# Attention and MoE on one core: a third operand set for head 2, staging for heads 1 and 2 in the x ring, and other plan numbers

## The chip, the core and the metric

One Trainium2 chip, one of its cores. A core has TensorE (PE, with its weight loads shown as PEld), VectorE (DVE), ScalarE (ACT), GpSimd (POOL) and SyncE (SP), which here issues nearly all DMA transfers. The metric is the device time of the whole program in microseconds, from several runs; the profile comes from one execution.

## What is computed

The kernel is an attention layer with a block mask, followed by a two-layer MoE-like block, all in fp32:

```python
scores = scale * np.matmul(q, k.transpose(0, 1, 3, 2))      # 4 batches, 8 heads, 768 x 64
scores = np.where(mask, scores, -1000000000.0)              # blocks of 32: band, first, last, 3 drawn
scores = scores - np.max(scores, axis=-1, keepdims=True)
attn = np.exp(scores)
attn = attn / (np.sum(attn, axis=-1, keepdims=True) + 1e-09)
out = np.matmul(attn, v)
# x: 3072 tokens x 512 (heads side by side)
h = x @ w_in                                                # 512 x 2048
g = np.where(h >= 1, h, np.where(h <= -1, 0.0, (h + 1) ** 2 / 4.0))
y = g @ w_out                                               # 2048 x 512
```

The weights come as 64-bit floats, and the kernel turns their bits into fp32 on the chip ("conversion").

## The kernel before

There are 32 heads (4 batches of 8), and after each batch the MoE block of that batch, which runs beside the next batch's heads. A head works on 768 x 768 scores in 12 chunks of 128 keys by 384 queries (`scores`, `expo`, `values`); its row maxima come first, from 12 matmuls (`max_mm`) that DVE reduces (`max_red`), then a column of maxima (`max_col`), a transpose on PE (`max_turn`) and a row that ACT or DVE writes into the operand (`max_row`). To keep fp32 accuracy an operand is split into a rounded part and a residual: `hi` rounds the loaded 128 x 768 tile `qk` into `qkh` on ACT, `lo` subtracts, and DMA moves (`hi_one`, `hi_two`, `lo_two`) put the four pieces into `KA`, `QA`, `KB` and `QB`. `KA` and `QA` exist twice (`SETS = 2`) and also hold the mask rows; heads take them in turn. `qk` and `qkh` have one buffer, `KB` and `QB` two. The x ring (`xp`, 10 buffers of 128 x 2 x 384) holds the attention output that feeds the MoE block.

Heads 0 to 9 (`WHOLE`) multiply the probabilities by the values in plain fp32 (L360); later heads split the probabilities too (L203, L343, L362, L363). The first batch is "wide": it may use the accumulators `oa0` to `oa2` and `hp` of the MoE block, which are free then.

The conversion of the weights works on pieces of 128 x 1024: L175 on ACT, then L176, L177, L179 and L181 on DVE, then a rounding on ACT (L203) and a residual on DVE (L187). `w_in` has eight pieces and stays in `wi`; `w_out` has eight pieces, is used by the first MoE half as it is made (tile `w`) and kept in DRAM for the later ones.

The order is set by a plan: every step is put into a list with a number (`at(t, ...)`), in units of one chunk, 12 units a head. Head i starts at 12 i; the steps ahead of it and behind it stand at distances from tables: `P` for all, `PW` over it for the first batch, `PA` for the second, `PM` for the first MoE half. `CONV` and `CSTEP` place the `w_in` conversions. The list is sorted and recorded, and a scheduler makes each engine's order from it, with the number as priority. Each engine then runs its own queue in order.

## Time and profile before

| | before |
|---|---|
| time, median of 3 runs | 975.48 us (972.75 to 977.56) |
| the profiled execution's own time | 975.02 us |
| its span | 973.2 us |
| PE busy | 946.3 us (97%) |
| DVE busy | 728.3 us (75%) |
| ACT busy | 645.0 us (66%) |
| POOL busy | 245.6 us (25%) |
| mean DMA rate | 158 GB/s |

Busy time of PE is the union of its matmuls, whose ends are modelled: two matmuls that start 0.18 us apart show 0.34 us each. So the starts tell its pace, and the rows that name a wait tell where it stood. A stretch of the span is read for itself: an engine that is busy three quarters of the span can be full in one head and idle in the next.

### The profile page before, as it was taken

To read this page: it belongs to the slowest core of one execution; us is meant where nothing else is said; L and a number is where in the kernel's file an instruction comes from. 1 tells how busy PE (TensorE), PEld (TensorE's weight loads), DVE (VectorE), ACT (ScalarE), POOL (GpSimd) and SP (SyncE) were. 2 spreads that over 40 slices of the span, in tenths; PEclk is the share of its full clock that TensorE was granted. 3 is DMA by queue.
4 is the path that set the end of the run, shared out by engine and by line. 5 is a ranking of instruction groups with operands and counts; after the bars stand their busy time and mean duration, and the time that the engine had idled before them with its cause. 6 is when DMAs were issued, how large, how long until landed. Compare 5 with 4: busy or idle time off the path is not lost.

```text
span 973.2 us, 14591 instructions
## 1 busy us (share of the span) xinstructions
PE 946.3 (97%) x4746; PEld 832.7 (86%) x4746; DVE 728.3 (75%) x1317; ACT 645.0 (66%) x1304; POOL 245.6 (25%) x230
## 2 busy tenths in 40 slices
PE   6899999998999999999999999999999999999998
PEld 4577777887889999998998999899899999999997
DVE  6889887779998888889887878888787885422222
ACT  5587876687676767767676676767667667433433
POOL 2000000024443334334333343433434344000000
PEclk9899999999999999999999999999999999999999
DMA  7766676653364555544464544545455432433432
GB/s 210 207 193 201 194 241 219 226 190 115 130 187 144 159 160 147 169 134 137 141 187 150 152 128 133 174 149 158 150 151 162 144 96 92 157 126 130 162 130 98
DMA packets 56080, 154.08 MB, mean 158 GB/s; under 512 B 9594, under 2 KB 17934, under 8 KB 56004
## 3 DMA queue, kind: packets, MB, share of 16 engines
q1 hardware_dynamic: 55964, 153.11, 51.1%
q8 instruction: 38, 0.62, 0.3%
q14 instruction: 38, 0.31, 0.1%
q10 hardware_dynamic: 40, 0.03, 0.0%
HBM read 100.95 MB, written 14.81 MB: 119 GB/s over the span
## 4 chain that ended last, share of the span: by engine, by line
PE 83%; DVE 7%; DMA 4%; issue 2%; ACT 2%; SPq 0%; ACTq 0%; DVEq 0%
PE oa L512 8%; PE oa L514 8%; PE oa L513 8%; PE hp L484 7%; PE hp L486 7%; PE hp L485 7%; PE pa L279 6%; PE pa L330 5%; PE po L362 5%; PE pa L331 5%; PE po L363 4%; PE po L360 4%; PE oa L360 3%; DVE mc L284 2%; DMA qk<-in_qk_t_dram 2%
## 5 line engine op out<-in xcount | busy, mean ns | idle before, releaser
L350 POOL TENSOR_TENSOR acc<-acc,pt 128x384 f32<-128x384 f32 x176 | 195.2, 1109 | 233.9 <-ACT pt L335 200.9
L284 DVE TENSOR_REDUCE mc<-pa 128x1 f32<-128x384 f32 x384 | 201.6, 548 | 20.1 <-PE pa L279 15.2
L203 ACT CAST ph<-pt 128x384 fp32r<-128x384 f32 x264 | 135.7, 514 | 92.9 <-PE po L362 86.3
L343 DVE TENSOR_TENSOR pl<-pt,ph 128x384 fp32r<-128x384 f32 x264 | 156.1, 591 | 37.1 <-ACT ph L203 36.5
L335 ACT ACTIVATE pt<-pa 128x384 f32<-128x384 f32 x288 | 140.6, 489 | 54.4 <-PE pa L331 44.2
L484 PE MATMUL hp<-x,wi 128*128 128x384 f32 x448 | 156.6, 349 | 2.3 <-DVE r L496 2.2
L512 PE MATMUL oa<-w,gh 128*128 128x512 f32 x384 | 153.8, 401 | 0.3 <-ACT gh L203 0.3
L514 PE MATMUL oa<-w,gl 128*128 128x512 f32 x384 | 151.6, 395 | 0.0
L486 PE MATMUL hp<-x,wi 128*128 128x384 f32 x448 | 151.6, 338 | 0.0
L485 PE MATMUL hp<-x,wi 128*128 128x384 f32 x448 | 151.1, 337 | 0.0
L513 PE MATMUL oa<-w,gh 128*128 128x512 f32 x384 | 150.8, 393 | 0.0
L279 PE MATMUL pa<-KA,QA 88*128 88x384 f32 x384 | 139.5, 381 | 2.1 <-DMA QA<-qkh 0.6
L350 POOL TENSOR_TENSOR acc<-pt 128x384 f32<-128x384 f32 x44 | 45.1, 1025 | 344.8 <-ACT pt L335 344.8
L496 DVE SCALAR_TENSOR_TENSOR r<-r,hp 128x384 f32<-128x384 f32 x112 | 61.7, 551 | 84.6 <-ACT r L493 84.4
L505 DVE TENSOR_TENSOR gl<-r,gh 128x384 fp32r<-128x384 f32 x128 | 89.9, 702 | 26.0 <-ACT gh L203 25.5
L490 ACT ACTIVATE r<-hp,half_c 128x384 f32<-128x384 f32 x112 | 65.1, 582 | 54.6 <-PE hp L486 47.7
L330 PE MATMUL pa<-QA,KA 102*128 102x384 f32 x288 | 98.9, 343 | 1.3 <-DVE mc L284 0.9
L331 PE MATMUL pa<-QB,KB 128*128 128x384 f32 x288 | 97.9, 340 | 0.0
L362 PE MATMUL po<-ph,vn 128*128 128x384 f32 x264 | 91.1, 345 | 3.0 <-DVE xun L372 2.8
L484 PEld LDWEIGHTS hp<-x,wi 128*128 128x128 f32 x448 | 84.5, 189 | 8.2 <-DVE r L496 4.0
L279 PEld LDWEIGHTS pa<-KA,QA 88*128 88x128 f32 x384 | 73.4, 192 | 21.0 <-DVE mc L284 6.0
L363 PE MATMUL po<-pl,vn 128*128 128x384 f32 x264 | 88.8, 337 | 0.0
(103 smaller groups left out, 1619.4 us busy)
## 6 DMA issues: line engine op xcount, KB each, us to landing
w<-wo_dram SPq DMA_DIRECT2D x112, 512.0 KB
qk<-in_qk_t_dram SPq DMA_DIRECT2D x32, 384.0 KB
raw<-in_moe_w_in_dram SPq DMA_DIRECT2D x16, 512.0 KB
raw<-in_moe_w_out_dram SPq DMA_DIRECT2D x16, 512.0 KB
wo_dram<-w SPq DMA_DIRECT2D x16, 512.0 KB
lv<-in_v_dram SPq DMA_DIRECT2D x32, 192.0 KB
QB<-qkh SPq DMA_DIRECT2D x32, 192.0 KB
KB<-qkh SPq DMA_DIRECT2D x32, 192.0 KB
```

The lines of the kernel that those rows point to most:

```text
L279: nc.tensor.matmul(out=pm[:, 0:HALF], lhsT=QAi[0:KM, t * 128:(t + 1) * 128], rhs=KAi[0:KM, kh * HALF:(kh + 1) * HALF], start=True, stop=True)
L284: nc.vector.reduce_max(out=st["mc"][:, t, kh:kh + 1], in_=st.pop(("pm", t, kh))[:, 0:HALF], axis=AX.X)
L330: nc.tensor.matmul(out=ps[:, 0:HALF], lhsT=KAi[0:KA, ks], rhs=QAi[0:KA, cs], start=True, stop=False)
L331: nc.tensor.matmul(out=ps[:, 0:HALF], lhsT=st["KB"][:, ks], rhs=st["QB"][:, cs], start=False, stop=True)
L343: (nc.gpsimd if i < 2 * H and c in PL1 else nc.vector).tensor_tensor(out=pl, in0=st["p", c], in1=f(st["ph", c]), op=ALU.subtract)
L350: nc.gpsimd.tensor_tensor(out=st["acc", hf], in0=prev, in1=st["p", c], op=ALU.add)
L484: nc.tensor.matmul(out=hv, lhsT=wi[:, j, 0, fs], rhs=x[:, 0], start=(j == 0), stop=False)
L485: nc.tensor.matmul(out=hv, lhsT=wi[:, j, 0, fs], rhs=x[:, 1], start=False, stop=False)
L486: nc.tensor.matmul(out=hv, lhsT=wi[:, j, 1, fs], rhs=x[:, 0], start=False, stop=(j == NP - 1))
L512: nc.tensor.matmul(out=o, lhsT=gh[:, ts], rhs=w[:, 0], start=(fi == 0), stop=False)
L513: nc.tensor.matmul(out=o, lhsT=gh[:, ts], rhs=w[:, 1], start=False, stop=False)
L514: nc.tensor.matmul(out=o, lhsT=gl[:, ts], rhs=w[:, 0], start=False, stop=(fi == NF - 1))
```

## The change

The x ring is empty until the first heads are done. The change uses eight of its ten buffers before that: two become a third pair `QA[2]`, `KA[2]`, used by head 2 alone; heads 1 and 2 load their `qk` into two more, right behind the constants, round into two more, and head 2's `KB` and `QB` take the last two. Heads from 3 on take the two old sets in turn (`operand_set`). The constant rows of sets 1 and 2 are written by GpSimd in a step of their own, `other_sets`. The residual `lo` is done by GpSimd for heads 1, 3, 5 and 6 (`QL`) and by DVE for the others; before it was GpSimd for head 0 alone. Heads 0 to 3 get tables of their own (`P0` to `P3`), all other tables have other numbers, and the `w_in` conversions start a little later and stand 2 x 7.19 units apart instead of 2 x 6.297.

```diff
+    def wide_tile():
+        return xp.tile([128, 2, HALF], F32R, name="x").rearrange("p a c -> p (a c)")
+
+    QA.append(wide_tile())
+    KAt.append(wide_tile())
+
+    def operand_set(i):
+        return i if i < 3 else (i - 3) % 2
...
-        for i in range(SETS):
+        for i in range(SETS + 1):
             nc.gpsimd.memset(f(QA[i][64:128]), 0.0)
...
-        for i in range(1, SETS):
-            rounded(nc.gpsimd, KAt[i][64:KA], ef)
         nc.scalar.copy(out=idr, in_=idf)
+        shared["ef"] = ef
+
+    def other_sets():
+        for i in range(1, SETS + 1):
+            rounded(nc.gpsimd, KAt[i][64:KA], shared["ef"])
+        rounded(nc.gpsimd, QA[SETS][64:KM], f(QA[0][64:KM]))
...
-        G = {**P, **PW} if wide else {**P, **PA} if i < 2 * H else P
+        G = {**P, **PW, **(P0, P1, P2, P3, {})[min(i, 4)]} if wide else {**P, **PA} if i < 2 * H else P
...
-        QAi, KAi = QA[i % SETS], KAt[i % SETS]
+        QAi, KAi = QA[operand_set(i)], KAt[operand_set(i)]
...
-            st["x"] = ld.tile([128, S], F32, name="qk")
+            st["x"] = f(wide_tile()) if i in (1, 2) else ld.tile([128, S], F32, name="qk")
...
-            st["hi"] = tp.tile([128, S], F32R, name="qkh")
+            st["hi"] = wide_tile() if i in (1, 2) else tp.tile([128, S], F32R, name="qkh")
...
-            (nc.vector if i else nc.gpsimd).tensor_tensor(out=st["x"], in0=st["x"], in1=f(st["hi"]), op=ALU.subtract)
+            (nc.gpsimd if i in QL else nc.vector).tensor_tensor(out=st["x"], in0=st["x"], in1=f(st["hi"]), op=ALU.subtract)
...
-            st["KB"] = qk.tile([128, S], F32R, name="KB")
-            st["QB"] = qk.tile([128, S], F32R, name="QB")
+            st["KB"] = wide_tile() if i == 2 else qk.tile([128, S], F32R, name="KB")
+            st["QB"] = wide_tile() if i == 2 else qk.tile([128, S], F32R, name="QB")
...
-        at(-99 if i == 0 else pre - G["qs"] - G["ld"], load_qk)
+        at((-99, -89, -88)[i] if i < 3 else pre - G["qs"] - G["ld"], load_qk)
...
     at(TC, consts)
+    at(TC2, other_sets)
...
+P2 = {'qs': 28.491, 'ld': 9.372, 'vs': 8.581, 'm0': 9.353, 'm1': 4.82, 'mr': 0.376, 'mc': 4.207, 'mt': 3.273, 'mw': 1.003, 'lag': 3.06}
+QL = (1, 3, 5, 6)
...
-CONV, CSTEP = 8.526, 6.297
+CONV, CSTEP = 8.718, 7.19
```

What this does to the engines' queues is shown at three places. First SP, which issues the transfers, from the loads and moves of the first heads on. Before, behind the constants, head 0's moves and two weight loads, this stands in a row (`qk_181` and `qkh_233` are head 1's):

```order
L217 DMA lv_356<-in_v_dram 128x384
L221 DMA qk_181<-in_qk_t_dram 128x768
L168 DMA raw_372<-in_moe_w_in_dram 128x1024 x2
L231 DMA KA1_116<-qkh_233 64x768
L231 DMA QA1_114<-qkh_233 64x768
L231 DMA QB_245<-qkh_233 64x768
L231 DMA KB_244<-qkh_233 64x768
L249 DMA QB_245<-qk_181 64x768
L250 DMA KB_244<-qk_181 64x768
L168 DMA raw_539<-in_moe_w_in_dram 128x1024 x2
L221 DMA qk_282<-in_qk_t_dram 128x768
```

Now the same place, ahead of any weight load (`x_162` and `x_164` are the loads of heads 1 and 2, `x_180` the rounded tile of head 1; `qk_126` is head 0's):

```order
L236 DMA x_162<-in_qk_t_dram 128x768
L236 DMA x_164<-in_qk_t_dram 128x768
L246 DMA QB_175<-qkh_168 64x768
L246 DMA KB_174<-qkh_168 64x768
L264 DMA QB_175<-qk_126 64x768
L265 DMA KB_174<-qk_126 64x768
L232 DMA lv_196<-in_v_dram 128x384
L246 DMA KA1_116<-x_180 64x768
L246 DMA QA1_114<-x_180 64x768
L246 DMA QB_193<-x_180 64x768
L246 DMA KB_192<-x_180 64x768
L264 DMA QB_193<-x_162 64x768
```

Both loads went ahead of head 0's moves; head 1's moves follow at once, then head 1's `lv` load and head 2's six moves, and only then the first two weight loads, of which four stood among these transfers before.

Second, PE from the end of head 0 to head 1's first score. Before (`KA_116`, `QA_114` are head 1's set; `oa_390` receives its first scores):

```order
L360 MATMUL oa_352<-pl,vn 128x384
L360 MATMUL oa_352<-pt,vn 128x384
L279 MATMUL pa<-KA_116,QA_114 128x384
L360 MATMUL oa_352<-ph,vn 128x384
L279 MATMUL pa<-KA_116,QA_114 128x384 x2
L360 MATMUL oa_352<-pl,vn 128x384
L279 MATMUL pa<-KA_116,QA_114 128x384 x6
L294 MATMUL pa<-idr,mr 1x128 x6
L330 MATMUL oa_390<-QA_114,KA_116 128x384
```

Now (`oa_396` receives head 1's first scores):

```order
L294 MATMUL pa<-KA_116,QA_114 128x384
L345 MATMUL oa_372<-QA_113,KA_115 128x384
L346 MATMUL oa_372<-QB,KB 128x384
L375 MATMUL oa_380<-pt,vn 128x384
L345 MATMUL oa_382<-QA_113,KA_115 128x384
L309 MATMUL pa<-idr,mr 1x128 x6
L346 MATMUL oa_382<-QB,KB 128x384
L375 MATMUL oa_380<-ph,vn 128x384
L345 MATMUL hp<-QA_113,KA_115 128x384
L346 MATMUL hp<-QB,KB 128x384
L375 MATMUL oa_380<-pl,vn 128x384
L345 MATMUL oa_396<-QA_114,KA_116 128x384
```

Head 1's maxima moved from the end of head 0 to its middle: the transposes stand among head 0's last scores, and three of head 0's last values come behind head 1's first score.

Third, DVE between head 8's last reduction and head 9's first. Before:

```order
L181 SCALAR_TENSOR_TENSOR cva_1753<-raw_1541,cva_1753 128x1024
L288 TENSOR_TENSOR mr_1525<-mc_1444 128x6
L399 RECIPROCAL rc_1512<-rc_1512 24x32
L240 TENSOR_TENSOR qk_1504<-qk_1504,qkh_1571 128x768
L176 TENSOR_SCALAR cva_1901<-cva_1901 128x1024
L177 TENSOR_SCALAR cva_1901<-cva_1901 128x1024
L179 SCALAR_TENSOR_TENSOR cva_1901<-raw_1635,cva_1901 128x1024
L181 SCALAR_TENSOR_TENSOR cva_1901<-raw_1635,cva_1901 128x1024
L187 TENSOR_TENSOR w_1819<-cva_1753,w_1819 128x512
```

Now:

```order
L191 TENSOR_SCALAR cva_1579<-cva_1579 128x1024
L303 TENSOR_TENSOR mr_1517<-mc_1436 128x6
L192 TENSOR_SCALAR cva_1579<-cva_1579 128x1024
L194 SCALAR_TENSOR_TENSOR cva_1579<-raw_1447,cva_1579 128x1024
L414 RECIPROCAL rc_1503<-rc_1503 24x32
L196 SCALAR_TENSOR_TENSOR cva_1579<-raw_1447,cva_1579 128x1024
L255 TENSOR_TENSOR qk_1486<-qk_1486,qkh_1565 128x768
L191 TENSOR_SCALAR cva_1718<-cva_1718 128x1024
L192 TENSOR_SCALAR cva_1718<-cva_1718 128x1024
L194 SCALAR_TENSOR_TENSOR cva_1718<-raw_1541,cva_1718 128x1024
L202 TENSOR_TENSOR w_1638<-cva_1579,w_1638 128x512
L196 SCALAR_TENSOR_TENSOR cva_1718<-raw_1541,cva_1718 128x1024
```

Two whole conversions stand here where one and a rest stood, and the piece of `w` in it is the first of the second weights; before it was the third.

## Rows read from the trace of the kernel before

**Rows 1.** The page, part 2: busy tenths of PE in 40 slices of the span

```profile
PE   6899999998999999999999999999999999999998
```

**Rows 2.** Chain that ended last, in order of time: start us, us, what; 0 to 60

```profile
0.74 2.92 DMA qk<-in_qk_t_dram
...
27.30 5.70 DVE mc L284 x12
...
36.60 7.42 DMA QA<-qkh
...
46.13 0.18 PE oa L330
...
46.66 0.65 PE po L360 x2
```

**Rows 3.** Timeline of PE, 25 to 45: start us, us, instruction [idle before <-releaser]

```profile
25.67 0.69 PE L279 MATMUL pa<-KA,QA 88*128 88x384 f32 x3
...
29.45 2.65 PE L279 MATMUL pa<-KA,QA 88*128 88x384 f32 x6
34.26 0.52 PE L294 MATMUL pa<-idr,mr 128*1 128x128 f32 x6 [2.16 <-DVE mr L288]
36.61 0.69 PE L330 MATMUL oa<-QA,KA 102*128 102x384 f32 x1 [1.83 <-ACT QA L299]
...
44.16 0.76 PE L279 MATMUL pa<-KA,QA 88*128 88x384 f32 x3 [0.63 <-DMA QA<-qkh]
```

**Rows 4.** Stretches: us, busy of PE, PEld, DVE, ACT, POOL; PEclk, DMA share, GB/s

```profile
35.00:41.83 6.83, 5.22 (x13) 4.32 (x14) 6.09 (x7) 5.05 (x10) 0.00 (x0) 0.50 0.79 183
58.70:136.10 77.40, 76.52 (x340) 56.92 (x339) 65.63 (x114) 61.92 (x121) 0.00 (x0) 1.00 0.72 212
136.10:151.30 15.20, 14.95 (x70) 11.28 (x68) 13.95 (x23) 11.05 (x22) 0.00 (x0) 1.00 0.68 215
151.30:179.70 28.40, 27.87 (x135) 23.00 (x134) 18.98 (x35) 18.91 (x38) 0.00 (x0) 1.00 0.71 227
211.50:242.80 31.30, 28.64 (x152) 26.00 (x151) 31.23 (x54) 24.87 (x52) 12.85 (x10) 1.00 0.39 124
```

The stretches are cut at the first maximum matmul of a head: heads 3 to 7, 8, 9 and 11.

**Rows 5.** Who PE waited for, 200 to the end: us in total, times, longest

```profile
PE po L362 <- DVE xun L372: 2.8, 4, 0.9
PE hp L484 <- DVE r L496: 2.2, 2, 1.7
PE pa L305 <- DVE mr L288: 1.4, 5, 0.3
```

**Rows 6.** Timeline of DVE, 7 to 12.2

```profile
7.18 0.55 DVE L120 CAST QA<-pa 24x384 fp32r<-24x384 f32 x1 [0.68 <-PE pa L118]
...
8.63 3.35 DVE L284 TENSOR_REDUCE mc<-pa 128x1 f32<-128x384 f32 x7
```

**Rows 7.** The residual `lo`, line 240: duration ns min/median/max, first and last start

```profile
L240 DVE TENSOR_TENSOR qk<-qk,qkh x31: 883/952/1770, 20.9 to 763.3; 128x768 f32<-128x768 f32 x31
...
L240 POOL TENSOR_TENSOR qk<-qk,qkh x1: 2072/2072/2072, 6.1 to 6.1; 128x768 f32<-128x768 f32 x1
```

**Rows 8.** Groups of DVE, 44.16 to 151.3: instruction xcount | busy us, mean ns

```profile
L179 DVE SCALAR_TENSOR_TENSOR cva<-raw,cva 128x1024 int32<-128x1024 int32 x8 | 9.8, 1224 | 0.2
L181 DVE SCALAR_TENSOR_TENSOR cva<-raw,cva 128x1024 int32<-128x1024 int32 x8 | 9.6, 1198 | 0.0
...
L176 DVE TENSOR_SCALAR cva<-cva 128x1024 f32<-128x1024 f32 x8 | 5.4, 672 | 0.5 <-ACT cva L175 0.4
```

**Rows 9.** Tile `w`, 130 to 250: duration ns min/median/max, first and last start

```profile
L512 PE MATMUL oa<-w,gh x36: 388/397/692, 160.5 to 247.5; 128*128 128x512 f32 x36
...
L187 DVE TENSOR_TENSOR w<-cva,w x14: 671/684/1504, 129.5 to 242.9; 128x512 fp32r<-128x512 f32 x14
```

**Rows 10.** Timeline of POOL and DVE around 344

```profile
343.76 1.17 POOL L350 TENSOR_TENSOR acc<-acc,pt 128x384 f32<-128x384 f32 x1 [0.67 <-ACT pt L335]
...
343.98 1.77 DVE L240 TENSOR_TENSOR qk<-qk,qkh 128x768 f32<-128x768 f32 x1
```

More of the change, by code (lines that the diff above doesn't have):

```diff
@@ L85, in body @@
     wi = cst.tile([128, 4, 2, FF], F32R, name="wi")
+    def wide_tile():
[4 more added lines that the diff above has]
+        return i if i < 3 else (i - 3) % 2
+    shared = {}
     def consts():
         M = slice(64, KM)
-        for i in range(SETS):
+        for i in range(SETS + 1):
             nc.gpsimd.memset(f(QA[i][64:128]), 0.0)
@@ L566, in body @@
         for hf in range(2):
-            moe(begin[b] + hf * NF * p, p, b, hf, b == 0 and hf == 0)
+            moe(begin[b] + (DELAY2 if b == 0 else 0) + hf * NF * p, p, b, hf, b == 0 and hf == 0)
     for fq in range(2):
@@ L586 @@
-PW = {'vw': 3.518, 'r1': 3.404, 'r2': 4.789, 'qs': 12.911, 'vs': 8.37, 'ld': 5.876, 'm0': 7.378, 'm1': 4.661, 'mr': 0.204, 'mc': 2.414, 'mt': 1.76, 'mw': 1.144, 'ex': 0.241, 'ph': 1.21, 'pl': 1.598, 'ps': 0.916, 'ow': 0.264, 'ot': -2.699, 'oa': 1.883, 'ah': 0.402, 'al': 1.005, 'su': 0.223, 'de': 0.736, 'yw': 0.447, 'yy': 1.398, 'xm': 0.574, 'xh': 0.586, 'xl': 1.764, 'lag': 3.338}
+P = {'vw': 5.936, 'r1': 0.432, 'r2': 3.59, 'qs': 8.759, 'ks': 11.973, 'vs': 8.74, 'ld': 6.54, 'm0': 8.319, 'm1': 5.436, 'mr': 0.733, 'mc': 1.81, 'mt': 1.788, 'mw': 0.322, 'ex': 0.098, 'ph': 0.947, 'pl': 1.297, 'ps': 1.153, 'ow': 1.181, 'ot': 0.059, 'oa': 0.704, 'ah': 0.495, 'al': 0.487, 'su': 0.524, 'de': 1.45, 'yw': -0.311, 'yy': 1.616, 'xm': 0.512, 'xh': 0.797, 'xl': 2.852, 'gr': 0.112, 'gs': 0.335, 'gm': 0.748, 'gh': 0.844, 'gl': 1.475, 'l2': 1.536, 'l3': 0.137, 'l1': 0.132, 'cl': 8.876, 'cs': 2.804, 'cd': 1.518, 'co': 6.416, 'lag': 3.517}
@@ new lines @@
+PW = {'vw': 2.912, 'r1': 3.203, 'r2': 4.396, 'qs': 12.314, 'vs': 8.121, 'ld': 6.69, 'm0': 8.627, 'm1': 4.668, 'mr': 0.184, 'mc': 1.989, 'mt': 1.714, 'mw': 1.232, 'ex': 1.044, 'ph': 0.99, 'pl': 2.083, 'ps': 2.834, 'ow': 0.042, 'ot': -5.45, 'oa': 2.183, 'ah': -0.339, 'al': 1.56, 'su': 0.973, 'de': 5.555, 'yw': 0.289, 'yy': -1.207, 'xm': 0.389, 'xh': 1.951, 'xl': 2.771, 'lag': 3.428}
+P0 = {'qs': 14.014, 'vs': 7.862, 'vw': 4.385, 'lag': 3.653}
+P1 = {'qs': 21.286, 'ld': 7.496, 'vs': 10.037, 'm0': 11.05, 'm1': 4.665, 'mr': 0.533, 'mc': 5.247, 'mt': 3.948, 'mw': 2.561, 'lag': 2.771}
@@ L587 @@
+P2 = {'qs': 28.491, 'ld': 9.372, 'vs': 8.581, 'm0': 9.353, 'm1': 4.82, 'mr': 0.376, 'mc': 4.207, 'mt': 3.273, 'mw': 1.003, 'lag': 3.06}
+P3 = {'qs': 13.489, 'ld': 3.031, 'vs': 8.426, 'm0': 9.569, 'm1': 5.068, 'mr': 0.299, 'mc': 4.038, 'mt': 3.742, 'mw': 3.153, 'lag': 3.444}
+QL = (1, 3, 5, 6)
 TC = -90
+TC2 = -13.843
+DELAY2 = 0.0
 ONE = 12
-XLATE = 2.917
-H0 = 0.909
+XLATE = 3.793
+H0 = 0.512
 PH1 = ()
@@ L595 @@
 XL1 = ()
-PA = {'vw': 5.512, 'r1': 0.547, 'r2': 4.117, 'qs': 10.75, 'vs': 6.462, 'ld': 4.892, 'm0': 7.743, 'm1': 5.228, 'mr': 0.143, 'mc': 2.394, 'mt': 1.652, 'mw': 1.455, 'ex': 0.059, 'ph': 1.335, 'pl': 1.842, 'ps': 1.512, 'ow': 0.661, 'ot': 0.022, 'oa': 0.543, 'ah': 0.931, 'al': -0.006, 'su': 0.132, 'de': 1.466, 'yw': 0.671, 'yy': 1.849, 'xm': -0.497, 'xh': 1.383, 'xl': 2.685, 'lag': 3.529}
-PM = {'gr': 0.185, 'gs': 0.223, 'gm': 1.002, 'gh': 1.663, 'gl': 1.759, 'l2': 1.57, 'l3': 0.114, 'l1': 0.131}
+PA = {'vw': 5.991, 'r1': 0.244, 'r2': 3.516, 'qs': 11.126, 'vs': 7.172, 'ld': 5.197, 'm0': 7.799, 'm1': 5.151, 'mr': 0.254, 'mc': 2.524, 'mt': 1.725, 'mw': 1.71, 'ex': 0.027, 'ph': 1.13, 'pl': 1.852, 'ps': 2.889, 'ow': 0.228, 'ot': 0.626, 'oa': 0.816, 'ah': 0.604, 'al': -0.517, 'su': 0.118, 'de': 1.21, 'yw': 0.563, 'yy': 1.92, 'xm': -0.801, 'xh': 0.497, 'xl': 2.418, 'lag': 3.504}
+PM = {'gr': -0.024, 'gs': 0.007, 'gm': 0.527, 'gh': 1.63, 'gl': 1.755, 'l2': 1.463, 'l3': 0.184, 'l1': 0.124}
 RINGS = {"s": ("oa0", "oa1", "hp"), "m": ("pa", "pa")}
-DELAY = 3.745
+DELAY = 3.792
 EARLY = 0
```

1 line of the change is left out of this document (removed).

## The prediction

> **What bounds the kernel now.** I read the busy digits of TensorE (PE) first, then the chain of waits, then PE's own rows around the holes, then the other engines head by head. The digits [rows 1] are full from the fifth slice on: for about 850 of 973 us the kernel is bound by PE, and a gain there would have to be fewer matmuls, which the change does not bring. The holes are in the first 45 us. The chain of the first 60 us [rows 2] names what fills them: twelve row maxima of head 1 on VectorE (DVE), 5.70 us, which start only at 27.30, and a 7.42 us transfer of head 2's Q into operand set 0. PE's rows [rows 3] show both from its side: at 29.45 six maximum matmuls take 2.65 us, paced by DVE, then 2.16 us go by until the column of maxima is there and 1.83 us until ScalarE (ACT) has written the row; at 44.16 the last 0.63 us of a wait for that transfer. Because PE had idled, its granted clock was 0.50, that is 1.2 GHz, from 35.00 to 41.83 [rows 4]. Later PE is held up little: from 200 us on its recorded waits are 2.8 us for the hand-over of `po`, 2.2 us for `r` and 1.4 us for `mr` [rows 5].
>
> **The change part by part.** The sum is made against the profiled execution: 975.0 us, span 973.2, 1.8 around it. The median of the three runs, 975.48, is 0.5 above; I leave that in the rounding.
>
> *Head 0.* Its first column of maxima now waits for six reductions and not seven: one reduction out of 3.35/7 = 0.48 us [rows 6], minus 0.48. The residual `lo` of head 0 goes from GpSimd to DVE, 0.95 us [rows 7], ahead of the two copies of the mask. DVE sits idle 0.68 us right there [rows 6], so 0.27 us stick out, and the second copy waits for ACT in any case: between 0 and +0.3, taken +0.1. Head 0: minus 0.4.
>
> *Between head 0 and head 1.* Head 1's Q and K are loaded right behind the constants. Head 0's load took 2.92 us [rows 2]; the two new ones queue behind it and each other, so I put them down by 8.5 us. ACT rounds head 1 once the masks are copied (about 9.2), SP issues its moves, and if each took as long as the worst one on record, 7.42 us [rows 2], they would be there at 17.5. Head 1's first maximum came at 25.67 [rows 3], by the order behind twelve scores; it now stands behind six, that is six chunks of 0.65 + 2 x 0.18 us [rows 2] earlier, about 19.6. No weight conversion is left on DVE ahead of head 1's reductions, so those run as soon as PE writes them, between head 0's scores. The stretch 29.45 to 36.61 [rows 3] is 7.16 us long and holds six maximum matmuls and six transposes, 6 x 0.18 + 6 x 0.06 = 1.4 us at the pitch of the undisturbed rows [rows 2]. The rest goes: minus 5.7. What comes next there is the row of maxima on ACT, which the new order gives three more chunks of head 0 as cover.
>
> *The clock.* In 35.00 to 41.83 PE was busy 5.22 us at half speed [rows 4]; without the hole ahead of it that work takes half: minus 2.6. The slow matmuls of head 0's own start stay.
>
> *Head 2.* It has an operand set and staging tiles of its own, so its moves wait neither for head 0's last matmul nor for a free `qk` or `qkh` buffer, and they are issued before the weight loads: minus 0.6 [rows 3]. In place of it the queue of SP gets a wait: head 1's `lv` load has to wait until ACT has copied head 0's `lv`, which stands behind the first exponential. Behind it stand head 2's moves and the first weight load. That copy is done at about 16 us and head 2's first maximum comes near 31, so even a move of 7.42 us [rows 2] is hidden.
>
> *What replaces the waits.* PE will not run without any hole where the old ones were; between 44 and 60 the chain still has short steps of ACT and DVE. I allow +0.7 (0 to +1.5).
>
> *Heads 3 to 7.* They took 77.40 us [rows 4]. PE's own work in that stretch is 62 chunks of 0.65 + 2 x 0.18, 60 maxima of 0.18 and 30 transposes: 74.3 us. At most 3.1 us can go. The number of conversions in it does not change (five); two residuals of it, those of heads 5 and 6, go to GpSimd, so DVE loses 2 x 0.95 us of its 65.6 [rows 4, 7]. Taken: minus 0.5 (minus 3.1 to 0).
>
> *Heads 8 and 9, the price.* "Later" has to land somewhere. By the order, ten conversions stand ahead of head 8's maxima and twelve ahead of head 10's; now it is seven and twelve. So heads 8 and 9 get, in pieces, three more of L176, L177 and L179, one more of L181 and two half ones of L187: 3 x (0.67 + 0.67 + 1.22) + 1.20 + 2 x 0.68 = 10.2 us, L177 counted like L176 [rows 8, 9]. DVE was busy 13.95 + 18.98 = 32.9 of the 43.6 us of those heads [rows 4]; now it is 43.1 of 43.6. Does that fit? Head 11 shows DVE at 31.23 of 31.30, so the bound below is +0. Heads 3 to 7 ran at 65.6/77.4 = 85%, which would make 50.8 us, +7.2: the bound above. The nearest row is head 8's own, 13.95/15.20 = 92%: 47.0 us, +3.4, which I take.
>
> *Heads 10 to 31 and the MoE halves* keep their instructions; the plan numbers alone change. By the order, PE has 3.6 us of work between a head's last maximum and its transpose, against 2.9 before, and the same 1.8 to 2.0 us between the last use of `po` and its next. So of the 1.4 us of waits for `mr` [rows 5] I take half off, minus 0.7, and nothing else; bounds minus 1.4 and +3.
>
> Sum: -0.4 - 5.7 - 2.6 - 0.6 + 0.7 - 0.5 + 3.4 - 0.7 = -6.4, so 975.0 - 6.4 = 968.6 us.
>
> **A rule that speaks against it.** One DVE row shows the two engines in each other's way: a residual on DVE took 1.77 us where the median is 0.95, with a GpSimd addition lying over its start [rows 7, 10]. For heads 3, 5 and 6 the residual is now a GpSimd instruction of about 2.07 us [rows 7] over a busy DVE; at 1.77 - 0.95 = 0.8 us for each such meeting that is 2.5 us of DVE time, inside the 11.8 us that DVE is idle in heads 3 to 7, so the sum has nothing for it. The Trainium skill (SBUF — State Buffer, section "Who interferes with whom") says that a VectorE instruction with two SBUF inputs and a GpSimd instruction that reads SBUF exclude each other for the whole instruction. By that rule each of the three could hold DVE up for all its length; the row agrees in kind, with a part of the length.
>
> **The rivals.**
> *B, the conversions fill heads 8 and 9.* DVE reaches only the 85% of heads 3 to 7 there: +7.2 in place of +3.4, 972.4 us. For it: ACT, which starts and ends each conversion, stands in DVE's chain. Against it: head 11.
> *C, the lock.* Each of the three residuals on GpSimd stops DVE for 2.07 us [rows 7] and PE behind it: +6.2, 974.8 us. Against it: DVE's idle time there.
> *D, slower.* The first MoE half, in heads 8 to 12, uses each piece of the second weights as it is made. Before, the first piece was written at 129.5 and first used at 160.5 [rows 9], 31 us of lead; now its conversion stands between head 8's and head 9's maxima, with 8 us of PE work left. If PE waits for each of the eight pairs as long as for the late `r`, 1.7 us [rows 5], that is +13.6: 982.2 us. It decides, in the sense of slower by over 0.5%, from seven of the eight pairs on (11.8/1.7). Against it: eight conversions are 40 us of DVE work and have some 90 us.
> *E, the change does not get its early start.* Moves of head 1 or 2 land more than 10 us after their issue, the holes of [rows 3] stay: 975 us. Against it: the 7.42 us above was behind a 512 KB load, and such loads now come later.
>
> **How the numbers follow.** Forecast 0.68, B 0.17, C 0.05, D 0.07, E 0.03. The forecast alone spans 964 to 972. The best of all bounds is 975.0 - 14 = 961; the worst without D is 975.0 - 9 + 7.2 + 3 = 976. The range leaves out D and the far end of the gains: 963.5 to 976. A measurement of this kernel tells a difference of about 0.5%, 4.9 us, from none, so faster means under 970.6: 0.60 out of the forecast and 0.06 out of B make 0.66; the same holds what else is in the forecast, B, C and E, 0.27; slower is D, 0.07.
>
> **What would show it.** In the trace after: head 1's first score near 29 us (36.61 before) and head 2's first maximum without a wait for a transfer; granted clock 1.00 from 20 us on; head 8's first maximum near 127 us (136.1 before). If head 10's first maximum comes less than 5 us earlier than 179.7, the price in heads 8 and 9 was higher than taken; if DVE there is below 92% and PE waits for `w`, D is at work. A PE wait for KA, QA or x before 60 us would mean E. If the gain at head 8 is there and the end is not earlier, the new plan numbers cost it after 200 us, and the waits for `po`, `mr` and `r` must have grown.

## The result and the profile after

The changed kernel takes 964.44 us (median of 4 runs, 961.11 to 966.29), the kernel before on the same chip 974.87: a ratio of 0.9888, interval 0.9850 to 0.9926. The profiled execution took 965.23 us with a span of 963.4, against 975.02 and 973.2. A second timing beside other kernels gave 964.62 us and 0.9887 (0.9861 to 0.9912).

**The holes of the first 45 us are gone.** PE's timeline of the changed kernel, 20 to 31 us (start us, us, instruction):

```profile
20.77 0.56 PE L294 MATMUL pa<-KA,QA 88*128 88x384 f32 x2
...
27.96 0.52 PE L309 MATMUL pa<-idr,mr 128*1 128x128 f32 x6
...
29.55 0.81 PE L375 MATMUL oa<-pl,vn 128*128 128x384 f32 x2
29.91 0.63 PE L345 MATMUL oa<-QA,KA 102*128 102x384 f32 x1
```

Head 1's maxima start at 20.77 inside head 0's scores, its transposes at 27.96, its first score at 29.91; these were 25.67, 34.26 and 36.61 with two waits of about 2 us [rows 3]. No row of this stretch carries a wait. The stretches that answer to [rows 4] (busy of PE, PEld, DVE, ACT, POOL; PEclk, DMA share, GB/s; cut at the first maxima of heads 3, 8, 9 and 10):

```profile
35.00:41.83 6.83, 6.83 (x32) 5.44 (x30) 6.50 (x13) 4.04 (x9) 0.00 (x0) 1.00 0.15 47
49.90:132.30 82.40, 79.77 (x350) 59.65 (x348) 67.56 (x113) 62.14 (x123) 4.73 (x2) 0.98 0.71 203
132.30:146.80 14.50, 14.44 (x67) 11.20 (x68) 13.69 (x24) 12.26 (x24) 0.00 (x0) 1.00 0.58 172
146.80:176.10 29.30, 28.52 (x134) 22.87 (x133) 27.80 (x45) 22.62 (x43) 0.00 (x0) 1.00 0.88 271
84.84:88.25 3.41, 3.41 (x10) 2.49 (x9) 2.10 (x5) 0.91 (x3) 0.00 (x0) 0.50 0.76 201
238.44:241.85 3.41, 3.41 (x12) 3.41 (x11) 2.28 (x5) 1.74 (x4) 1.13 (x1) 0.50 0.83 286
```

Where 13 matmuls ran at half clock, 32 run at full clock. Heads 8 and 9 take 43.8 us (43.6 before) although DVE works 41.5 us in them (32.9 before). But heads 3 to 7 took longer, 82.4 against 77.4, and two stretches at half clock are new: 10 matmuls in 3.41 us from 84.84, and 12 from 238.44.

First maxima mislead here, since the new numbers also move the maxima ahead of the scores. So I use another measure: PE runs the same 4746 matmuls in both kernels. Each kind has its undisturbed pitch (the lower decile of its start-to-start times in the kernel before; the plain fp32 values, whose starts come in uneven pairs, count about 0.32 us each; 906.4 us in all). **Lateness** is the start of a matmul minus the pitches of all matmuls ahead of it: it grows only when PE stands or runs slowly. The stretch of heads 3 to 7 is work 46 to 118.5, heads 8 and 9 end at 171:

```
PE work done, us        12      20      46      60      70     118.5    171     300     925
lateness before, us    13.08   21.63   22.75   23.89   24.26   26.52   28.96   38.68   62.78
lateness after, us     14.29   14.64   16.66   16.46   20.33   22.27   25.17   36.26   52.96
after minus before     +1.2    -7.0    -6.1    -7.4    -3.9    -4.2    -3.8    -2.4    -9.8
```

Single steps hang on the choice of pitches by some 0.3 us; the differences at 300 and at the end do not. The last column is the whole result: 975.0 - 9.8 = 965.2. It was made in two places: 8.2 us at once where head 1 starts, and 7.4 us in small pieces behind work 300; between them 4.6 us were lost again. The loss of 3.5 us from 60 to 70 is a single event, head 5's Q. SP's queue, then chain and PE of the changed kernel:

```profile
76.21 0.34 SPq L183 DMA_DIRECT2D raw<-in_moe_w_in_dram  x1
76.64 0.47 SPq L246 DMA_DIRECT2D KA<-qkh  x1
77.17 0.59 SPq L246 DMA_DIRECT2D QA<-qkh  x1
```

```profile
75.17 0.83 ACT qkh L218
...
77.17 6.18 DMA QA<-qkh
83.48 0.76 PE pa L294 x3
```

```profile
83.48 0.76 PE L294 MATMUL pa<-KA,QA 88*128 88x384 f32 x3 [1.68 <-DMA QA<-qkh]
```

The move is issued behind a 512 KB weight load and takes 6.18 us; PE waits 1.68 us, and 1.36 us after it resumes its clock is at half for 3.41 us (in the repeat below the half clock began 0.17 us before PE resumed). Behind 200 us the wait for `mr` [rows 5] is gone from PE's list, that for `po` is 1.9 in place of 2.8, that for `r` 1.6 in place of 2.2 (in total, times, longest):

```profile
PE po L377 <- DVE xun L387: 1.9, 2, 1.2
PE hp L499 <- DVE r L511: 1.6, 2, 1.4
PE oa L527 <- ACT gh L218: 0.3, 1, 0.3
PE pa L294 <- DVE mc L299: 0.2, 1, 0.2
```

### The profile page after: what moved, and what is told of

Read it like the earlier page. It is cut to its first block, busy times and chain, and to the rows that moved or that the text cites. A ratio compares the mean times of both kernels' runs of the same rounds, so it can differ in the third digit from the quotient of the medians.

```text
span 963.4 us, 14639 instructions
## 1 busy us (share of the span) xinstructions
PE 941.9 (98%) x4746; PEld 834.5 (87%) x4746; DVE 728.1 (76%) x1314; ACT 641.1 (67%) x1304; POOL 264.1 (27%) x236
## 4 chain that ended last, share of the span: by engine, by line
PE 91%; DVE 3%; ACT 2%; DMA 2%; issue 1%; POOL 0%; SPq 0%; ACTq 0%; DVEq 0%
PE oa L527 9%; PE oa L529 9%; PE oa L528 9%; PE hp L500 8%; PE hp L501 8%; PE hp L499 8%; PE pa L294 7%; PE pa L345 5%; PE pa L346 5%; PE po L377 5%; PE po L378 5%; PE po L375 4%; PE oa L375 2%; PE pa L501 1%; PE pa L500 1%
## 5 line engine op out<-in xcount | busy, mean ns | idle before, releaser
L365 POOL TENSOR_TENSOR acc<-acc,pt 128x384 f32<-128x384 f32 x176 | 203.0, 1154 | 222.8 <-ACT pt L350 181.4
L358 DVE TENSOR_TENSOR pl<-pt,ph 128x384 fp32r<-128x384 f32 x264 | 163.3, 620 | 30.4 <-ACT ph L218 29.0
L294 PE MATMUL pa<-KA,QA 88*128 88x384 f32 x372 | 134.1, 377 | 4.5 <-DMA QA<-qkh 2.6
L511 DVE SCALAR_TENSOR_TENSOR r<-r,hp 128x384 f32<-128x384 f32 x112 | 61.8, 551 | 83.5 <-ACT r L508 82.4
L520 DVE TENSOR_TENSOR gl<-r,gh 128x384 fp32r<-128x384 f32 x128 | 78.3, 612 | 20.5 <-ACT gh L218 20.1
```

Of the source, the lines that this page charges most:

```text
L294: nc.tensor.matmul(out=pm[:, 0:HALF], lhsT=QAi[0:KM, t * 128:(t + 1) * 128], rhs=KAi[0:KM, kh * HALF:(kh + 1) * HALF], start=True, stop=True)
L358: (nc.gpsimd if i < 2 * H and c in PL1 else nc.vector).tensor_tensor(out=pl, in0=st["p", c], in1=f(st["ph", c]), op=ALU.subtract)
L365: nc.gpsimd.tensor_tensor(out=st["acc", hf], in0=prev, in1=st["p", c], op=ALU.add)
```

## The experiments

My theory after the comparison: the plan numbers of the later heads carry some 7 us by themselves and the early part about 4, after giving back what heads 3 to 7 lose. The rival: all of it comes from the early part, which hands the later heads a lead. All ratios below are to the kernel before, timed on the same chip.

### Which half of the change carries it

*The plan numbers alone, in the kernel before:*

```diff
-P = {... 'mc': 2.424, 'mw': 1.353, ... 'cl': 10.585, ...}
+P = {... 'mc': 1.81, 'mw': 0.322, ... 'cl': 10.585, ...}
-PA = {... 'mw': 1.455, ...}
+PA = {... 'mw': 1.71, ...}
-PM = {... 'gm': 1.002, ...}
+PM = {... 'gm': 0.527, ...}
```

> The kernel before with the changed kernel's plan numbers for heads 10 to 31 and the MoE parts (PA, PM and P without the four conversion keys); sets, staging, the first heads and the conversions stay as before. In the changed kernel heads 13 to 31 gained about 7 us over the kernel before and TensorE's waits for the row of maxima and its idle time in 290 to 830 us were halved (14.0 to 6.8 us). Theory 1, those plan numbers alone carry it: minus 5 to minus 8 us, 967 to 970, with head 13's first maximum within 1.5 us of 272.2 and head 30's 5 to 8 us ahead of 753.8. Theory 2, the later heads gain because the early part hands them a lead and other conversions: within 1.5 us of the kernel before, 973.5 to 976.5.

Measured: 972.16 us, 0.9960 (0.9939 to 0.9982). Between the two theories: minus 3.9 us by the medians. Head 13's first maximum at 273.5 and head 30's at 750.3 (3.5 ahead). From work 300 to the end its lateness grows by 21.0 us, against 24.1 before and 16.7 after.

*The same with three more numbers:*

```diff
-XLATE = 2.917
-H0 = 0.909
-DELAY = 3.745
+XLATE = 3.793
+H0 = 0.512
+DELAY = 3.792
```

> The kernel before with all numbers of the changed kernel that act on heads 8 to 31 and the MoE parts: as in the run of the plan numbers alone, and besides H0, XLATE and DELAY. That run took 4.2 us off heads 16 to 30 where the changed kernel took 7.4 off. Theory 1, the rest of it sits in these three numbers: heads 16 to 30 in 390.5 to 392.5 us (398.5 in the kernel before, 391.1 in the changed one), the whole 968 to 970. Theory 2, the rest is scatter between executions, or comes from the other parity of the operand sets: heads 16 to 30 stay at 393.5 to 396 and the whole at 971 to 973.

Measured: 970.41 us, 0.9958 (0.9944 to 0.9973), minus 4.5. Heads 16 to 30 took 392.2 us, as theory 1 has it; the whole came 0.4 above its range. Lateness from 300 on: 17.7, nearly that of the changed kernel. That it is the three numbers, and not scatter between executions, the two times can't tell: their intervals overlap almost wholly. The next run points the same way: it has the three numbers beside the old `P`, `PA` and `PM`, and from 300 on its lateness grows by 21.8 us, 2.3 less than in the kernel before.

*The early part without the new plan numbers (`XLATE`, `H0` and `DELAY` stay new):*

```diff
-P = {... 'mc': 1.81, 'mw': 0.322, ... 'cl': 8.876, ...}
+P = {... 'mc': 2.424, 'mw': 1.353, ... 'cl': 8.876, ...}
-PA = {... 'mw': 1.71, ...}
+PA = {... 'mw': 1.455, ...}
-PM = {... 'gm': 0.527, ...}
+PM = {... 'gm': 1.002, ...}
```

> The changed kernel with the kernel before's plan numbers for heads 10 to 31 and the MoE parts (PA, PM and P without the four conversion keys); the third operand set, the staging tiles, the first heads' numbers and the later conversions stay. Theory 1, the early part is worth what is left of it at head 13 (2.7 us): minus 2 to minus 4.5 us, 970.5 to 973, with a first maximum of head 3 near 50 us (58.7 before) and head 13's near 269.5. Theory 2, the gain of the later heads comes from the early part: minus 9 to minus 11 us, 964 to 966.

Measured: 968.25 us, 0.9922 (0.9908 to 0.9935), minus 7.9: neither range. Head 3's and head 13's first maxima came at 49.9 and 267.4. The gap to the kernel before at work 300 is 4.9 us and at the end 7.3.

So both halves count, and neither theory had the sizes. The two runs that split the change between them, the first and this one, bring 3.9 and 7.9 us, 11.8 together, where the changed kernel has 10.4; the intervals are too wide to call the difference real. The 4.5 us of the run between them can't be added to the 7.9, since both have the three numbers. What the new numbers remove shows in who PE waits for, 290 to 830 us. First the run with the early part and the old `P`, `PA`, `PM`, then the kernel before with all the new numbers, then the changed kernel (in total, times, longest):

```profile
PE pa L320 <- DVE mr L303: 2.0, 7, 0.3
PE pa L345 <- DVE mc L299: 0.7, 3, 0.2
PE pa L294 <- ACT pt L350: 0.3, 1, 0.3
```

```profile
PE po L362 <- DVE xun L372: 1.4, 2, 0.7
```

```profile
PE po L377 <- DVE xun L387: 0.7, 1, 0.7
```

The waits for the maxima (`mr`, `mc`) stand there in every kernel of the study with the old `P` and in none with the new. The waits for `po` vary from kernel to kernel, 0 to 3.3 us, with either set.

### The tiles without the numbers, the numbers without the tiles

*Third set, staging tiles, `other_sets` and `QL` as changed; `P`, `PW`, `PA`, `PM`, `XLATE`, `H0`, `DELAY`, `CONV` and `CSTEP` as before, and:*

```diff
-P0 = {'qs': 14.014, ...}
+P0 = {}
...
-P3 = {'qs': 13.489, ...}
+P3 = {}
```

> The third operand set, the staging tiles, the early loads of heads 1 and 2, the constants' own step and the residuals on GpSimd as in the changed kernel, but every plan number that existed before as before, conversions included, and no numbers of their own for heads 0 to 3. Theory 1, the tiles only make an earlier start possible and the numbers make it happen: conversions still stand ahead of head 1's maxima, head 1's first maximum stays at 24 to 27 us, head 3's at 55 to 59, the whole 972 to 976. Theory 2, the tiles by themselves free head 1 and head 2: head 3's first maximum at 50 to 53, the whole 968 to 971.

Measured: 976.58 us, 1.0016 (0.9997 to 1.0034): no gain. Head 1's and head 3's first maxima came at 25.3 and 56.4, as theory 1 has it; the time came 0.6 above its range. PE waits where it waited before, and DVE (second fence) has conversions there:

```profile
35.89 0.52 PE L309 MATMUL pa<-idr,mr 128*1 128x128 f32 x6 [3.63 <-DVE mr L303]
```

```profile
32.21 1.22 DVE L196 SCALAR_TENSOR_TENSOR cva<-raw,cva 128x1024 int32<-128x1024 int32 x1
33.34 1.02 DVE L299 TENSOR_REDUCE mc<-pa 128x1 f32<-128x384 f32 x2
34.53 1.23 DVE L202 TENSOR_TENSOR wi<-cva,wi 128x1024 fp32r<-128x1024 f32 x1 [0.18 <-ACT wi L218]
35.67 0.16 DVE L303 TENSOR_TENSOR mr<-mc 128x6 fp32r<-128x6 f32 x1
```

*The numbers without the tiles:*

```diff
-    QA.append(wide_tile())
-    KAt.append(wide_tile())
...
-        return i if i < 3 else (i - 3) % 2
+        return i % SETS
```

> The changed kernel without the third operand set and the staging tiles: heads 1 and 2 load and round in the ordinary buffers, head 2 shares set 0; all plan numbers, the later conversions and the residuals on GpSimd stay. Theory 1, the extra tiles are what lets head 2 in early: TensorE waits for head 2's transfer until head 0's last score is over, and behind that wait SP's queue holds the weight loads; plus 3 to plus 7 us over the changed kernel, 967.5 to 971.5, head 3's first maximum 53 to 58 us. Theory 2, the numbers for the first four heads alone do it, the tiles are not needed: within 1.5 us of the changed kernel.

Measured: 988.71 us, 1.0133 (1.0115 to 1.0150). This run doesn't answer the question cleanly: with two sets, head 2's moves are recorded ahead of head 0's scores into the same tiles, so head 0's scores are computed from head 2's Q and K, and PE waits for that move in the middle of head 0 and again at head 1:

```profile
21.94 1.30 PE L290 MATMUL pa<-KA,QA 88*128 88x384 f32 x3 [5.16 <-DMA QA<-qkh]
...
36.59 0.66 PE L341 MATMUL oa<-QA,KA 102*128 102x384 f32 x1 [5.06 <-DMA QA<-qkh]
```

What it does show: these numbers for heads 1 and 2 can't be had with two sets. The numbers need the tiles, and the tiles alone bring nothing. Whether the first heads' own numbers or the later conversions carry the gain was not tested apart.

### Head 5's Q, and what heads 3 to 7 give back

*The changed kernel again, and a kernel with the moves a chunk earlier:*

> The changed kernel once more, beside the three others of this call, for two questions. Its stretches at half clock stood at 84.84 and 238.44 us, each 3.41 us long; one of the runs with residuals on VectorE had neither, though TensorE waited 2.65 us for the same move of head 5. Theory 1, these stretches follow from the waits ahead of them, which the order sets: both come again within 1 us of their places. Theory 2, whether a wait of this size costs the clock differs between executions: one or both are missing, and head 16's first maximum comes 2 to 4 us ahead of 352.0. The whole: 962 to 967.

Measured: 964.62 us; half clock from 83.62 and from 237.22, each 3.41 us, both 1.22 us earlier, just outside theory 1's 1 us; its first heads run 0.8 us earlier too. Both come back near the same places of the work, which favours theory 1, though two executions can't rule out theory 2 (see the second stretch below).

```diff
-PW = {... 'qs': 12.314, ...}
+PW = {... 'qs': 13.314, ...}
```

> The changed kernel with one number changed: the first batch's qs from 12.314 to 13.314, so that the casts and moves of heads 4 to 7 are issued about a chunk and more earlier and head 5's moves stand ahead of two weight loads in SP's queue, not behind. In the changed kernel head 5's QA move was issued at 77.17, took 6.18 us beside a 512 KB load, TensorE waited 1.7 us for it and ran 3.41 us at half clock from 84.84. Theory 1, the queue place is the cause: no wait for QA at head 5, clock 1.00 there, head 6's first maximum 3 to 4 us ahead of 100.9, the whole 961 to 963. Theory 2, the move is late because its cast or its free operand set is late, not its place: the wait stays over 1 us and the time is within 1.5 us of the changed kernel.

Measured: 982.64 us, 1.0075 (1.0056 to 1.0094). Inconclusive: at this number the moves of heads 4 to 7 are recorded ahead of the last scores of heads 2 to 5, so these last scores read the next user's operands, and PE waits for the moves there (`hp` from `QA<-qkh`, 4.6 us in two waits).

*One weight piece set to zero by GpSimd in place of two loads (its values are left out of the computation):*

```diff
-                Q_RAW.dma_start(out=st["raw"][:, k * 512:(k + 1) * 512],
-                                in_=src[k].bitcast(I32).rearrange("p (c w) -> p c w", w=2))
+                nc.gpsimd.memset(f(st["raw"][:, k * 512:k * 512 + 512]), 0.0) if 57 < t - P["cl"] < 58 else Q_RAW.dma_start(...)
```

> The changed kernel with one 128x1024 piece of the first weights (the fifth to be converted) not loaded but set to zero by GpSimd, so that two loads of 512 KB are gone from SP's queue ahead of head 5's moves; this leaves that piece's values out of the computation, the conversion's arithmetic stays. Theory 1, head 5's wait for QA and what follows it come from these loads, by the transfer time and by SP's place behind them: no wait over 0.5 us for QA at head 5, no half clock near 85, head 6's first maximum 2.5 to 4.5 us ahead of that of the changed kernel, the whole 1.5 to 4 us less. Theory 2, the cast on ACT and the denominator's transfers ahead in SP's queue hold it: the wait stays over 1 us, and head 6 within 1 us.

Measured: 969.16 us, 0.9943 (0.9923 to 0.9964). The mechanism is theory 1's: head 5's Q move takes 3.05 us, PE does not wait for it, no half clock near 85. The value is not: head 6's first maximum comes at 100.4, 0.7 ahead of the repeat's 101.1, and over heads 3 to 7 lateness grows by 6.3 us, against 5.6 and 5.2 in the two executions of the changed kernel. From work 60 to 70 alone it grows by 1.2 us, against 3.9 and 4.9: the local loss is gone, and other waits came in its place behind it. PE of this run:

```profile
84.63 0.44 PE L294 MATMUL pa<-KA,QA 88*128 88x384 f32 x1 [0.66 <-DVE mc L299]
...
94.36 0.45 PE L345 MATMUL oa<-QA,KA 102*128 102x384 f32 x1 [1.48 <-ACT QA L314]
```

In the chain of this run DVE's conversion steps and the row of maxima stand ahead of these; the scheduler had sorted the steps anew. That the new order made the loss is read from these rows, not tested by itself.

*Residuals of heads 3, 5 and 6 on VectorE:*

```diff
-QL = (1, 3, 5, 6)
+QL = (1,)
```

> The changed kernel with the residuals of heads 3, 5 and 6 back on VectorE (head 1's stays on GpSimd); order up to there unchanged. In the changed kernel they are GpSimd instructions of 1.83, 2.04 and 2.69 us, and beside the last one a VectorE instruction of 1.2 us took 2.75. Theory 1, the two engines lock each other and that is part of the 5 us which heads 3 to 7 give back: minus 1 to minus 3 us against the changed kernel at head 8's first maximum (132.3). Theory 2, VectorE has idle time there, the lock is covered and the extra 0.95 us each would not matter either: within 1 us at head 8. Theory 3, VectorE is full in heads 3 to 7 and GpSimd relieved it: plus 1 to plus 4 us at head 8.

Measured: 967.25 us, 0.9921 (0.9902 to 0.9940), about 3 us above the changed kernel, with intervals that overlap. Head 8's first maximum came at 129.1, 3.2 earlier, which looks like theory 1 (131.1 in the repeat of the changed kernel); but its first score came at 140.7 (141.5 and 140.2 in the two executions of the changed kernel), and lateness over heads 3 to 7 grew by 6.5 us. The maxima were only sorted ahead. So taking the lock away in this manner, which gives VectorE the three residuals as work, gives nothing back. This run waits longer for head 5's Q, yet keeps the full clock (PE, then the stretch behind it):

```profile
83.46 0.77 PE L294 MATMUL pa<-KA,QA 88*128 88x384 f32 x3 [2.65 <-DMA QA<-qkh]
```

```profile
83.46:90.00 6.54, 6.54 (x30) 5.42 (x31) 6.00 (x12) 4.27 (x8) 0.00 (x0) 1.00 0.65 191
```

From work 60 to 70 lateness grows by 3.2 us here (15.46 to 18.69), with 2.65 of waiting; by 4.9 in the repeat, with 2.8, and by 3.9 in the changed kernel, with 1.7, both with the half clock. Without the waits that is 0.5 us here and 2.1 to 2.2 in the other two: the half clock itself costs about 1.6 us, near half of its 3.41 us. Why this wait was spared stays open.

### The start, and the lock between VectorE and GpSimd

*Head 0's residual back on GpSimd:*

```diff
-QL = (1, 3, 5, 6)
-TC2 = -13.843
+QL = (0, 1, 3, 5, 6)
+TC2 = -13.5
```

> The changed kernel with head 0's residual lo back on GpSimd, issued ahead of the extra sets' constants. In the changed kernel it ran on VectorE for 1.47 us beside a GpSimd addition and head 0's first maximum came at 8.72 us (7.88 before). Theory 1, that residual on VectorE delays the mask copies and all behind them: first maximum near 7.9, head 1's first score about 0.8 us earlier than 30.9, the whole 0.5 to 1.0 us shorter. Theory 2, the lateness comes from something else at the start (constants, clock): first maximum stays at 8.5 or later and the time within 0.5 us of the changed kernel.

Measured: 972.42 us, 0.9963 (0.9948 to 0.9977), by the ratios some 7 us above the changed kernel, and the first maximum at 10.0. Both theories are wrong. VectorE and GpSimd of this run:

```profile
4.91 3.06 DVE L120 SCALAR_TENSOR_TENSOR al<-cmt,sf,al 24x24 f32<-24x24 f32 x3
8.01 0.17 DVE L125 TENSOR_SCALAR mb<-al 24x24 fp32r<-24x24 f32 x1
```

```profile
5.23 0.83 POOL L216 TENSOR_SCALAR KA<-raw 38x768 fp32r<-38x768 f32 x1 [1.57 <-DVE al L120]
6.14 1.80 POOL L255 TENSOR_TENSOR qk<-qk,qkh 128x768 f32<-128x768 f32 x1
```

Three operations on 24 x 24 elements, 0.78 us in the run below, took 3.06: the second of them ended at 6.08, when GpSimd's copy of constant rows ended (6.06), the third at 7.97, when GpSimd's residual ended (7.94). In the kernel before they were done before that residual began. Here VectorE's chain began 0.4 us later than in the changed kernel (4.05 against 3.65, behind the load of `qk`), and that put them beside GpSimd; whether other executions of this run have the meeting is not known. The rest of the loss is not this lock: the run's lateness is 2.4 us above the changed kernel's at work 46, 5.6 at 171 and 9.4 at the end, in an order of the first heads that was sorted anew (a wait of 2.5 us for `QA`, one of 1.7 for `mr`, a stretch at half clock from 70.54).

*The third set's constant rows on ACT:*

```diff
-            rounded(nc.gpsimd, KAt[i][64:KA], shared["ef"])
+            rounded(nc.gpsimd if i < SETS else nc.scalar, KAt[i][64:KA], shared["ef"])
```

> The changed kernel with the constant rows of the third set's KA written by ACT, which waits 1.94 us there, and not by GpSimd, so that head 0's residual on VectorE has no GpSimd instruction beside it. In the changed kernel that residual took 1.47 us beside an addition on GpSimd (0.95 us is the median). Theory 1, the two engines held each other up: the residual takes 0.9 to 1.0 us, head 0's first maximum comes at 8.0 to 8.3 us (8.72). Theory 2, its length comes from something else (the tile just written by ACT, the transfers of the start): 1.3 us or more again, first maximum 8.6 or later. The whole, either way, within 3 us of the changed kernel, since the scheduler then sorts the first heads' steps anew.

Measured: 971.15 us, 0.9956 (0.9941 to 0.9971). The local part is theory 1's. The residual in the changed kernel, and in this one:

```profile
6.53 1.47 DVE L255 TENSOR_TENSOR qk<-qk,qkh 128x768 f32<-128x768 f32 x1
```

```profile
4.67 0.78 DVE L120 SCALAR_TENSOR_TENSOR al<-cmt,sf,al 24x24 f32<-24x24 f32 x3
...
6.66 0.96 DVE L255 TENSOR_TENSOR qk<-qk,qkh 128x768 f32<-128x768 f32 x1
```

0.96 us without GpSimd beside it, and the first maximum at 8.3. That time by itself shows little: the repeat of the changed kernel has 8.3 as well, with a residual of 1.47 us in a chain that began earlier. Nor does the gain reach PE. Its first wait for `mr` grew from 0.90 us (at 12.58 in the changed kernel) to 1.64:

```profile
13.14 0.48 PE L309 MATMUL pa<-idr,mr 128*1 128x128 f32 x3 [1.64 <-DVE mr L303]
```

Lateness at work 12 is 14.3 us in both. The whole is 6.5 us worse than the changed kernel, twice what I had allowed for the re-sorting: lateness is level with it at work 20 (14.48) and 2.3 above at 60 (18.80), with new waits of 0.6 and 1.1 us for `pl` from ACT between. A local gain of 0.5 us was lost many times over.

### The second stretch at half clock

```diff
-PA = {... 'mw': 1.71, ...}
+PA = {... 'mw': 1.455, ...}
-PM = {... 'gm': 0.527, ...}
+PM = {... 'gm': 1.002, ...}
```

> The changed kernel with the kernel before's PA and PM (second batch and first MoE half); P, PW, P0 to P3 and the rest as changed. With the old P, PA and PM together head 13's first maximum came at 267.4 (269.5 in the changed kernel) and the half clock at 238.4 to 241.8 was not there, while heads 16 to 30 took 4.7 us more. Theory 1, PA and PM cost 2 us in heads 8 to 13 and P gives the gain behind: 961.5 to 963.5, no half clock around 240. Theory 2, that half clock comes and goes between executions or hangs on P: within 1.2 us of the changed kernel.

Measured: 965.77 us, 0.9901 (0.9880 to 0.9923): the same as the changed kernel, not theory 1's gain of 1 to 3 us. No half clock around 240; lateness from work 200 to 215 grows by 3.6 us where the changed kernel's grows by 5.7, and at 300 the run is 3.4 ahead.

That `PA` and `PM` set this half clock does not follow. The run with the tiles alone has the old `PA` and `PM` and a half clock from 241.68; the run with the residuals of heads 3, 5 and 6 on VectorE and the one with ACT have the new ones and none there. Ahead of that place the changed kernel and the run with these residuals on VectorE show the same two waits:

```profile
235.96 0.45 PE L499 MATMUL hp<-x,wi 128*128 128x384 f32 x1 [1.36 <-DVE r L511]
237.61 0.44 PE L377 MATMUL po<-ph,vn 128*128 128x384 f32 x1 [1.21 <-DVE xun L387]
```

```profile
235.83 0.44 PE L499 MATMUL hp<-x,wi 128*128 128x384 f32 x1 [1.36 <-DVE r L511]
237.49 0.44 PE L377 MATMUL po<-ph,vn 128*128 128x384 f32 x1 [1.22 <-DVE xun L387]
```

The pair stands in six executions with the new `PA` and `PM`; four of them ran 3.41 us at half clock from there and two did not, which is theory 2's "comes and goes". From work 200 to 215 the four grow by 5.6 to 5.7 us and the two by 4.1 to 4.2, so this stretch too costs about 1.5 us.

Of its lead of 3.4 us the run with the old `PA` and `PM` loses the larger part behind 500, with waits for `po` (its rows, 660 to 800; the changed kernel has none there):

```profile
PE po L377 <- DMA KB<-qk: 1.2, 1, 1.2
PE po L377 <- DVE xun L387: 0.7, 1, 0.7
```

Whether these waits belong to that order or to that execution stays open. No kernel of the study beats the changed one by more than the intervals allow.

## Why the prediction was right

The forecast was 968.6 us in a range of 963.5 to 976; it came to 964.4. The sign and the main mechanism held; four terms were mis-sized, partly against each other. That the sum stayed inside the range is partly luck: the first, third and fourth row below came out 4.7 us worse than forecast, the last two 8.2 better. Term by term, the measured side being the step in lateness of the profiled execution (in brackets the same in the repeat):

| stretch of PE's work | forecast | measured |
|---|---|---|
| head 0, to 12 | -0.4 | +1.2 (+0.4) |
| hole and half clock, 12 to 20 | -8.3 | -8.2 (-8.2) |
| head 2's transfer, new short waits, 20 to 46 | +0.1 | +0.9 (+0.8) |
| heads 3 to 7, 46 to 118.5 | -0.5 | +1.8 (+1.4) |
| heads 8 and 9, 118.5 to 171 | +3.4 | +0.5 (+0.4) |
| plan numbers, 171 to the end | -0.7 | -6.0 (-4.9) |
| sum | -6.4 | -9.8 (-10.1) |

*Head 0.* One reduction less was right: six stand ahead of the first `mr`. What failed is the price of the residual on DVE, "between 0 and +0.3": it took 1.47 us and not 0.95, because `other_sets` puts a copy of constant rows on GpSimd beside it. I had counted the moved residual and not what the new step puts on the neighbour. How much of the 1.2 us that is stays open: with the 0.5 us taken away, in the run with ACT, PE was as late. The term varies between executions (+0.2 in the run with the residuals of heads 3, 5 and 6 on VectorE, which is unchanged up to there), and the rows show with what: PE's starts stand 0.32 us apart until 20 us in the changed kernel's execution and until 17.6 in that one.

*The hole and the clock.* Read from [rows 3] and [rows 4], this term came out within what the measure can tell, and the run with the tiles alone fits its reason: with conversions still ahead of head 1's reductions the wait is 3.63 us. Head 1's first score was to come near 29 and came at 29.91. Head 2 waits for no transfer. Of the new short waits the longest is 1.1 us for ACT's row of head 2, ahead of 47.5; it names `x`, which by the letter of my sign would mean rival E, but what ended it is ACT and not a transfer. Two other signs failed: the clock was not 1.00 throughout (84.84, 238.44), and head 8's first maximum came at 132.3, not near 127.

*Heads 3 to 7.* The bounds were minus 3.1 to 0, and the term came out above them. (With the pitches as printed PE's own work there is 75.2 us, not 74.3, so 2.2 us could go; the term hardly hangs on it.) The step that failed is in rival E's "against": the 7.42 us of head 2's move was behind a 512 KB load, "and such loads now come later". They came later, and met head 5: 6.18 us, a wait of 1.68, then the half clock. I had used the lateness of the loads as a reason for the early heads and not asked whose moves they would stand in front of next. Taking the loads away took the wait away, but not the loss, so the wait is not all of what binds there.

*Heads 8 and 9.* The count was about right: 10.2 us more for DVE, 8.6 by the rows above. The rate was wrong. I took 92%, from head 8, between bounds of nothing and 7.2; DVE reached 95% (41.5 of 43.8), and the stretch hardly grew. The better row was head 11's, 31.23 of 31.30 [rows 4]: DVE can be full as long as PE has queued work that does not need it. Rival B falls with it, and D: the first piece of `w` was being written 9.7 us ahead of its first use (31 before), and PE never waited for `w` (durations, first and last start):

```profile
L527 PE MATMUL oa<-w,gh x36: 388/396/692, 156.4 to 245.6; 128*128 128x512 f32 x36
...
L202 DVE TENSOR_TENSOR w<-cva,w x14: 670/684/693, 146.7 to 239.5; 128x512 fp32r<-128x512 f32 x14
```

My reading rule, that a gain under 5 us at head 10's first maximum would mean a higher price in heads 8 and 9, was wrong too: it was 3.6, and the loss lay in head 5.

*The plan numbers.* The largest miss. The reason was the right one, more work between a head's last maximum and its transpose, so that `mr` is waited for less. But I halved the 1.4 us of [rows 5] and took the list for the whole. From 290 to 830 us PE's recorded idle time fell from 4.8 us to 0.7, all of `mr` and `mc` and part of `po`; the growth of lateness from work 300 on fell by more, 7.4 us, so matmuls that start late without a listed wait are in it too. Undone alone they cost some 3 us (0.9922 against 0.9888, intervals that overlap), put into the kernel before they bring 3.9, or 4.5 with the three numbers; so not all of the 6.0 need be theirs. My bounds, minus 1.4 to plus 3, were drawn around the list and too narrow below. The range had a slip as well: its upper end, 976, puts the early terms in at their forecast values, minus 9.1 together, and not at their upper bounds, which would add 1.5; it made no difference here.

*The rule on the lock* was priced at nothing for heads 3, 5 and 6, and that holds: with these residuals on VectorE the kernel is no faster. But the rows now show the lock in full, and at the start it costs VectorE 0.5 us, for which the sum had no term (last section). Rival C's price, 6.2 us for three residuals, was far too high: in the changed kernel's trace two of the three meet a VectorE operation, which takes 0.4 and 1.5 us longer, and beside the third VectorE had no work.

## What to carry to other kernels

A plan number and the buffer that allows it are one edit: here the tiles alone brought nothing and the numbers alone mixed the operands of two heads, and a step moved in time must be followed to the next transfer that its loads will stand in front of. To judge a bound engine, add up how late it is against its own undisturbed pace, stretch by stretch; a list of waits shows the few long ones, and the first use of one step misleads when the plan also moves that step. In an order that a scheduler sorts, expect a small local gain to be worth less than the re-sorting around it: two edits that took away a delay seen in the trace cost 4.5 and 6.5 us. And a half clock that comes in one execution and not in another, behind the same waits, is no evidence for an edit until it is seen in several.
